# Attention, a routed expert layer and a gated network in one kernel: gathers, copies and stores reordered around the experts, and a second PSUM tile for the attention's product

## The chip, the cores and the metric

One Trainium2 chip; the kernel runs on one of its cores. Time is device time in microseconds (us). Engines: PE (TensorE, matrix products), DVE (VectorE), ACT (ScalarE), POOL (GpSimd) and SP (SyncE, which issues DMAs). Each engine works through its own instructions in order and waits on semaphores for the others.

## The reference

Three layers, each on the result of the one before. N is 4608 tokens (8 batches of 576), 512 wide.

```python
# attention: q, k, v are (8, 8, 576, 64)
q_s = softmax(q, axis=-1)              # exp(q - max) / (sum + 1e-9)
k_s = softmax(k, axis=2)               # over the sequence
kv  = einsum('bhsd,bhse->bhde', k_s, v)
x   = einsum('bhsd,bhde->bhse', q_s, kv)      # then (4608, 512)
# routed experts: E = 8, F = 1024, two experts for each token
logits = x @ w_gate + log1p(exp(x @ w_noise)) * noise
top2   = the two largest of each row; top2_w = softmax over the two
x      = sum over the two: top2_w * (relu(x @ w1[e]) @ w2[e])
# gated network
out = ((x @ w1) * (x @ w2)) @ w3 @ w_out
```

## The kernel before

Large products are done in split form: each float32 operand is the sum of a rounded part and a remainder (split(), L93: one ACT copy, one DVE subtraction), and mm3() (L97 to L100) adds three products.

**Attention and routing (front(), L142 to L593).** Tokens go in 36 tiles of 128. For tile i, q_tr transposes (L336), q_exp takes the exponential (eqT, L340), q_mm multiplies with the batch's table (pm, L347 to L350), q_out normalises (qr L355, xn L358, lp L360, xt L363) and stores the rows to X in device memory (L366). pm is one PSUM tile of two banks. Between these steps k_step prepares the tables of later batches. route() works out, for groups of tiles, the two experts of each token and its place in their lists, by one-hot products (L406, L464). As long as no expert works (alone is true, until the first 18 tiles are routed), bank() gives the transposes banks of ptr and pyy in turn, two each, and the routing's sums the two banks of phh. Afterwards the experts have phh and bank() gives all of the front ptr and pyy. The order of instructions on each engine up to L872 comes from the framework's planner, from dependences, the order of the text and its estimates; from L872 on (manual_schedule) it is the order of the text.

**Experts.** Expert 0's first-half tokens are done beside the rest of the attention (units 0 and 1, na = 2), then experts 1 to 7 in four units each (units 2 to 29), then expert 0's second half (units 30 and 31; nu = 32). A unit is two or three tiles of 128 rows: product1 (eight steps fb, result to a bank named ph, emptied by ACT L738 and DVE L739 into hT), then product2 (row blocks m, bank py, emptied by ACT L749, stored to Y in device memory by a DMA that ACT issues, L751). The rows of a unit are gathered from X by indirect DMAs of POOL (L709, or L137 in four quarters). Up to unit 2, transp() first copies the gathered rows into another column order (G.tensor_copy, L122, into a tile of the two-buffer pool y, which also holds the rows on their way to Y), then PE transposes (L124); later units are transposed by DVE in 32 x 32 blocks (L117). A hook after each step converts weights of the gated network on DVE and ACT (L628 to L646).

**Gated network (gated(), L993).** Blocks of three tiles: eight steps fb with two products of 12 matmuls each, then three row blocks m. take(i) (L953) weighs and adds the two expert rows of tile i (L957, L960), transposes and splits them into xT, and issues gather2(i + 2). gather2(i) fetches both expert rows of tile i from Y, eight indirect DMAs of POOL, into pool g2 with four buffers, two tiles deep. In block b, take() of block b + 1 comes after fb = 1, fb = 5 and m = 0 (CFB). The first takes come through events: take(0) after step 9 of unit 30, take(1) after step 2 and take(2) after step 7 of unit 31 (steps 0 to 7 are fb, 8 on are m). columns(), after unit 5, clamps pos (L879), lets PE replicate pos and gw over the partitions (replicate, L127 to L133) and writes posq and gwq (L880, L882), which gather2 and take use.

Of the kernel before, what the change touches and what calls it, by code (L numbers as in the profile page):

```python
# [8 lines left out]
F32 = mybir.dt.float32  # L9
# [6 lines left out]
ALU = mybir.AluOpType  # L16
AX = mybir.AxisListType
PSUM = bass.MemoryType.PSUM
# [7 lines left out]
E = 8  # L26
# [10 lines left out]
RTAIL = 4  # L37
PUMP = 3
CFB = {1: 0, 5: 1, 8: 2}
GROUPS = [(0, 9), (9, 15), (15, 18), (18, 26), (26, 32), (32, 35), (35, 36)]  # L40


@with_exitstack
def moe_chain_kernel(ctx, tc, q, kt, v0, v1, noise, wg, w1, w2, mw1, mw2, mw3t, mwo, out):
# [4 lines left out]
    def pool(stack, name, bufs, **kw):  # L49
        return stack.enter_context(tc.tile_pool(name=name, bufs=bufs, **kw))  # L50
# [33 lines left out]

    def open_late():
        early.close()
        for name, bufs in (("w2", 4), ("ht", 1), ("xt", 2), ("xg", 3), ("y", 2)):
            late[name] = pool(main, name + "p", bufs, side="right", reuse_waits="tile")
    ptr = pool(main, "ptr", 2, space=PSUM)
    phh = pool(main, "phh", 2, space=PSUM)  # L90
    pyy = pool(main, "pyy", 2, space=PSUM)

    def split(src, hi, lo):  # L93
        A.copy(out=hi, in_=src)  # L94
# [4 lines left out]
        P.matmul(ps, st_h, mv_l, start=False, stop=False)  # L99
        P.matmul(ps, st_l, mv_h, start=False, stop=last)  # L100

    turns = {"ph": [phh], "py": [pyy]}

    def bank_of(kind, shape):
        pools = turns[kind]
# [5 lines left out]

        return rows.rearrange("p (i c d) -> p c i d", i=4, c=4)

    def transp(src, xt, t, quarters):
        if quarters:
            pt = extra["xq"].tile([128, 4, 4, 32], F32, name="xq", tag="xq")
            V.transpose(out=pt, in_=src.rearrange("p (j c d) -> p c j d", j=4, c=4))  # L117
            pt = pt.rearrange("p c j t -> p c (j t)")
        else:
            pt = ptr.tile([128, 4, 128], F32, name="pt", tag="pt")  # L120
            rows = late["y"].tile([128, 4, 4, 32], F32, name="xr", tag="y")
            G.tensor_copy(out=rows, in_=by_chunk(src))  # L122
            for c in range(4):
                P.transpose(pt[:, c, :], rows[:, c].rearrange("p i d -> p (i d)"), ident)  # L124
        split(pt, xt[:, 0, :, 128 * t:128 * t + 128], xt[:, 1, :, 128 * t:128 * t + 128])
# [16 lines left out]
    def front(st):  # L142
# [9 lines left out]
        kts, vs, ks_, eks, qs, eqs, xq = {}, {}, {}, {}, {}, {}, {}  # L152
        alone = [True, 0]

        def bank(shape, route=False):
            if alone[0]:
                if route:
                    return phh.tile(shape, F32, name="rb", tag="ph")
                alone[1] += 1
                pl, tg = ((ptr, "pt"), (pyy, "py"))[alone[1] % 2]  # L160
                return pl.tile(shape, F32, name="fb", tag=tg)
            alone[1] += 1
            if alone[1] % 3 == 0:
                return pyy.tile(shape, F32, name="rb", tag="py")
            return ptr.tile(shape, F32, name="pt", tag="pt")
# [174 lines left out]
            A.activation(out=eqT, in_=pts.pop(i), func=AF.Exp)  # L340

        def q_mm(i):
            pms[i] = pm = pmm.tile([128, 4, 256], F32, name="pm", tag="pm")
            b0, b1 = (i * 128) // S, (i * 128 + 127) // S
            for p in range(4):
                if b0 == b1:
                    P.matmul(pm[:, p, 0:162], eqs[i][:, p, :], tab[b0 % 3][:, p, :], start=True, stop=True)  # L347
                else:
                    P.matmul(pm[0:64, p, 0:162], eqs[i][:, p, 0:64], tab[b0 % 3][:, p, :], start=True, stop=True)
                    P.matmul(pm[64:128, p, 0:162], eqs[i][:, p, 64:128], tab[b1 % 3][:, p, :], start=True, stop=True)  # L350
# [20 lines left out]
        def onehots(i0, sl, cols, acc):  # L371
            n, kk = sl.shape[1], sl.shape[2]
            si = sm.tile([128, n, kk], I32, name="si", tag="si")
            V.tensor_copy(out=si, in_=sl)
            yield
            sj = sm.tile([128, n, kk], I32, name="sj", tag="sj")
            V.tensor_single_scalar(out=sj, in_=si, scalar=7, op=ALU.arith_shift_right)
            V.tensor_single_scalar(out=si, in_=si, scalar=127, op=ALU.bitwise_and)
            yield
            jf = sm.tile([128, n, kk], F32, name="jf", tag="jf")  # L380
            V.tensor_copy(out=jf, in_=sj)
            pf = sm.tile([128, n, kk], F32, name="pf", tag="pf")
            V.tensor_copy(out=pf, in_=si)
            yield
            per = 4 // kk
            for c0 in range(0, n, 2 * per):
                c1 = min(n, c0 + 2 * per)
                pl = bank([128, cols], True)
                for a in range(c0, c1, per):
                    z = min(c1, a + per)  # L390
                    m = (z - a) * kk
                    oa = sm.tile([128, 4, 128], F16, name="oa", tag="oa")
                    V.tensor_tensor(out=oa[:, 0:m], in0=iob[:, None, :].to_broadcast([128, m, 128]),
                                    in1=pf[:, a:z, :].rearrange("p n k -> p (n k)")[:, :, None].to_broadcast(
                                        [128, m, 128]), op=ALU.is_equal)
                    yield
                    ob = sm.tile([128, 4, cols], F16, name="ob", tag="ob")
                    V.tensor_tensor(out=ob[:, 0:m], in0=iob[:, None, 0:cols].to_broadcast([128, m, cols]),
                                    in1=jf[:, a:z, :].rearrange("p n k -> p (n k)")[:, :, None].to_broadcast(
                                        [128, m, cols]), op=ALU.is_equal)  # L400
                    obn = ob[:, 0:m].rearrange("p (n k) c -> p n k c", k=kk)
                    G.tensor_tensor(out=obn, in0=obn, in1=tag[:, i0 + a:i0 + z][:, :, None, None].to_broadcast(
                        [128, z - a, kk, cols]), op=ALU.mult)
                    yield
                    for j in range(m):
                        P.matmul(pl, oa[:, j], ob[:, j], start=(a == c0 and j == 0), stop=(z == c1 and j == m - 1))  # L406
                    yield
                if i0 + c0 in (0, HT):
                    V.tensor_copy(out=acc, in_=pl)
                else:  # L410
                    V.tensor_tensor(out=acc, in0=acc, in1=pl, op=ALU.add)
                yield
# [17 lines left out]
        def route(gi):  # L430
# [29 lines left out]
            m = sm.tile([128, n, E], BF16, name="m", tag="m")  # L460
            V.tensor_tensor(out=m, in0=oh[:, :, 0, :], in1=oh[:, :, 1, :], op=ALU.add)
            yield
            pr = bank([128, n, E], True)
            P.matmul(pr, upper, m, start=True, stop=False)  # L464
            P.matmul(pr, onesb, run[:, None, :].to_broadcast([128, n, E]), start=False, stop=(n == 1))
            for j in range(n - 1):
# [46 lines left out]
            yield  # L513
            V.tensor_tensor(out=gw[:, i0:i1, 1], in0=gw[:, i0:i1, 0], in1=w, op=ALU.mult)
            if i1 in (HT, NT):
                pc = bank([128, E], True)
                P.matmul(pc, onesb, run, start=True, stop=True)
                V.tensor_copy(out=cnt[:, half, :], in_=pc)
                yield
# [198 lines left out]
    def xpose(u, t):  # L718
        if t == 0:
            xts[u] = late["xt"].tile([128, 2, 4, 384], F32R, name="xT", tag="xT")  # L720
        transp(xg.pop((u, t)), xts[u], t, u > na)

    def turn(u, step):
        n, e, part, j0, nt, N, first, last = units[u]
# [151 lines left out]

    def columns():

        V.tensor_scalar(out=pos, in0=pos, scalar1=float(E * ROWS - 1), scalar2=None, op0=ALU.min)  # L879
        V.tensor_scalar(out=posq, in0=replicate(pos.rearrange("p n k -> p (n k)")), scalar1=4.0,  # L880
                        scalar2=quart[:, 0:1], op0=ALU.mult, op1=ALU.add)
        V.tensor_copy(out=gwq, in_=replicate(gw.rearrange("p n k -> p (n k)")))  # L882
# [62 lines left out]
    def gather2(i):  # L945
        if i >= NT:
            return
        for k in range(2):
            y = extra["g2"].tile([128, D], F32, name="yg", tag="yg")
            gather_quarters(y, Y, posq[:, :, 2 * i + k:2 * i + k + 1])  # L950
            x2s[i, k] = y

    def take(i):  # L953
# [8 lines left out]
        b, t = divmod(i, BT)  # L962
        if t == 0:
            xts["g", b] = late["xt"].tile([128, 2, 4, 384], F32R, name="xT", tag="xT")
        transp(y0, xts["g", b], t, True)
        gather2(i + 2)

    def load_b():
        for j in range(4):
# [1 line left out]

    nu = len(units)
    events[nu - 3, 7] = [w34_begin]
    events[nu - 2, 9] = [lambda: take(0)]
    events[nu - 1, 2] = [lambda: take(1)]
    events[nu - 1, 7] = [lambda: take(2), load_b]
    for u in range(na, nu):
# [3 lines left out]
            unit(u, hook_conv, True)  # L981
        if u == na:
            turns["py"].append(ptr)
        if u == na + 3:
            columns()
        if u == nu - 3:
            w34()
    for j in range(4):
        wscratch(("w", j), 20 + j, late["w2"])

    most = nc.values_load(nmax[0:1, 0:1], min_val=0, max_val=T)

    def gated():  # L993
        N = 128 * BT
        nblk = NT // BT
        ap_ = extra["a"]
        for b in range(nblk):
            xt = xts.pop(("g", b))
            pT = late["ht"].tile([128, 2, 8, 384], F32R, name="hT", tag="hT")
            for fb in range(8):  # L1000
                f0 = 128 * (fb % 2)
                for g in ("a", "b"):
# [8 lines left out]
                    else:  # L1011
                        V.tensor_tensor(out=a, in0=a, in1=ps, op=ALU.mult)  # L1012
                        split(a, pT[:, 0, fb, :], pT[:, 1, fb, :])
                if b + 1 < nblk and fb in CFB:
                    take(BT * (b + 1) + CFB[fb])
            for m in range(BT):
                po = bank_of("py", [128, 512])
                for fb in range(8):
# [4 lines left out]
                A.copy(out=y, in_=po)  # L1023
                r = N * b + 128 * m
                nc.sync.dma_start(out=out[r:r + 128, :], in_=y)
                if b + 1 < nblk and m + 8 in CFB:
                    take(BT * (b + 1) + CFB[m + 8])

    gated()
    main.close()  # L1030
# [125 lines left out]
```

## Time and profile before

| | us |
|---|---|
| median of 3 runs | 1745.32 (1743.0 to 1746.36) |
| the profiled execution | 1746.65 |
| its span, first to last instruction | 1744.7 |
| PE busy | 1665.7 (95%) |
| DVE busy | 886.3 (51%) |
| ACT busy | 572.5 (33%) |
| POOL busy | 690.7 (40%) |
| mean granted TensorE clock | 0.982 |

A row of a timeline has the start, the length and the instruction, with out<-in by the program's names; in brackets stands the time for which the engine was idle before it, and what released it. Matmuls are pipelined: their lengths overlap, and the distance between their starts is what one takes. The front takes about 230 us, units 2 to 29 go to about 1020 us, the product of w3 and w_out (w34) and units 30 and 31 to about 1131, and the gated network takes the rest.

### The profile page before, as it was taken

The numbers are of one execution on the slowest core, as the hardware profiler recorded it, in microseconds if no ns is written. First come the engines' busy times: TensorE is split into PE (matmuls) and PEld (weight loads), VectorE is DVE, ScalarE is ACT, GpSimd is POOL, SyncE is SP. The second block draws the span as 40 slices with busy tenths as digits, with TensorE's granted clock in tenths as the row PEclk, the third lists the DMA queues.
The fourth block names the chain that finished last, engine by engine and source line by source line (L and its number), as shares of the span: only waits on it lengthen the run. The fifth ranks groups of instructions, "written<-read, shape, count | busy, mean of one in ns | idle before, by whom it ended". The sixth has DMA issues, their size and how long they took to land. (4 is left out here: it accounts for less than half of the span.)

```text
span 1744.7 us, 26430 instructions
## 1 busy us (share of the span) xinstructions
PE 1665.7 (95%) x9903; PEld 1519.5 (87%) x9903; DVE 886.3 (51%) x2251; ACT 572.5 (33%) x1195; POOL 690.7 (40%) x706
## 2 busy tenths in 40 slices
PE   6887979989999999999999999899999999999998
PEld 5666868988989989899998988789999999999997
DVE  6699735766567575774767513233323233332321
ACT  6553322333233333332333312232223233232321
POOL 4456334414334143341443420544454454444500
PEclk9898989999999999999999999999999999999999
DMA  8875344535355253553545484521111111111100
GB/s 297 263 238 173 110 151 150 175 104 168 112 169 172 86 177 124 162 157 104 166 152 173 154 318 165 187 101 43 49 53 48 52 54 35 44 48 52 50 23 20
DMA packets 130060, 221.51 MB, mean 127 GB/s; under 512 B 18560, under 2 KB 65792, under 8 KB 126848
## 3 DMA queue, kind: packets, MB, share of 16 engines
q1 hardware_dynamic: 95040, 152.07, 26.7%
q0 software_dynamic: 19072, 39.88, 8.4%
q10 hardware_dynamic: 15808, 27.71, 4.3%
q8 instruction: 85, 1.39, 0.3%
q14 instruction: 55, 0.45, 0.1%
HBM read 152.22 MB, written 67.37 MB: 126 GB/s over the span
## 5 line engine op out<-in xcount | busy, mean ns | idle before, releaser
L98 PE MATMUL ph<-xT,w 128*128 128x384 f32 (+1 forms) x1792 | 576.2, 322 | 13.6 <-DVE hT L739 9.4
L99 PE MATMUL ph<-xT,w 128*128 128x384 f32 (+1 forms) x1792 | 574.6, 321 | 0.8 <-DVE xT L95 0.7
L100 PE MATMUL ph<-xT,w 128*128 128x384 f32 (+1 forms) x1792 | 574.0, 320 | 0.0
L137 POOL DMA_INDIRECT xg<-X,idxq x288 | 282.5, 981 | 467.7 <-DVE xq L117 395.3
L137 POOL DMA_INDIRECT yg<-Y,posq x288 | 295.0, 1024 | 364.9 <-DVE yg L960 209.0
L98 PEld LDWEIGHTS ph<-xT,w 128*128 128x128 f32 x1792 | 339.8, 190 | 18.6 <-DVE hT L739 11.8
L100 PE MATMUL py<-w,hT 128*128 128x512 f32 x904 | 353.0, 390 | 0.4
L99 PE MATMUL py<-w,hT 128*128 128x512 f32 x904 | 352.3, 390 | 0.0
L98 PE MATMUL py<-w,hT 128*128 128x512 f32 x904 | 352.2, 390 | 0.0
L99 PEld LDWEIGHTS ph<-xT,w 128*128 128x128 f32 x1792 | 339.4, 189 | 3.3 <-DVE xT L95 1.5
L100 PEld LDWEIGHTS ph<-xT,w 128*128 128x128 f32 x1792 | 339.5, 189 | 0.0
L100 PEld LDWEIGHTS py<-w,hT 128*128 128x128 f32 x904 | 169.7, 188 | 37.4 <-DVE hT L739 2.0
L99 PEld LDWEIGHTS py<-w,hT 128*128 128x128 f32 x904 | 169.7, 188 | 34.0
L98 PEld LDWEIGHTS py<-w,hT 128*128 128x128 f32 x904 | 169.7, 188 | 33.9
L1012 DVE TENSOR_TENSOR a<-a,ph 128x384 f32<-128x384 f32 x96 | 53.0, 552 | 281.6 <-PE ph L100 263.5
L739 DVE SCALAR_TENSOR_TENSOR hT<-ph,hT 128x256 fp32r<-128x256 f32 (+1 forms) x256 | 120.5, 474 | 103.4 <-ACT hT L738 100.4
L738 ACT ACTIVATE hT<-ph 128x256 fp32r<-128x256 f32 (+1 forms) x256 | 107.2, 426 | 158.1 <-PE ph L100 143.6
L95 DVE TENSOR_TENSOR xT<-xq,xT 128x512 fp32r<-128x512 f32 x108 | 74.8, 693 | 154.9 <-ACT xT L94 154.9
L749 ACT COPY y<-py 128x512 f32<-128x512 f32 x77 | 45.2, 587 | 258.0 <-PE py L100 214.4
L94 ACT CAST xT<-xq 128x512 fp32r<-128x512 f32 x108 | 67.0, 620 | 138.7 <-DVE xq L117 129.2
L94 ACT CAST hT<-a 128x384 fp32r<-128x384 f32 x96 | 49.4, 514 | 182.3 <-DVE a L1012 182.3
L95 DVE TENSOR_TENSOR w<-raw,w 128x1024 fp32r<-128x1024 f32 x72 | 88.8, 1236 | 11.7 <-ACT w L94 11.6
(203 smaller groups left out, 1529.5 us busy)
## 6 DMA issues: line engine op xcount, KB each, us to landing
raw<-in_w_dram SPq DMA_DIRECT2D x72, 512.0 KB, 4.1
w<-WS SPq DMA_DIRECT2D x24, 1024.0 KB, 6.6
WS<-hl SPq DMA_DIRECT2D x80, 256.0 KB, 2.8
Y<-y ACTq DMA_DIRECT2D x77, 256.0 KB, 2.5
k<-in_kt_dram SPq DMA_DIRECT2D x32, 288.0 KB, 4.4
q<-in_q_dram SPq DMA_DIRECT2D x36, 256.0 KB, 4.0
X<-xt SPq DMA_DIRECT2D x36, 256.0 KB, 2.4
out_dram<-y SPq DMA_DIRECT2D x36, 256.0 KB, 2.1
```

The source lines that it names most:

```text
L94: A.copy(out=hi, in_=src)
L95: V.tensor_tensor(out=lo, in0=src, in1=hi.bitcast(F32), op=ALU.subtract)
L98: P.matmul(ps, st_h, mv_h, start=first, stop=False)
L99: P.matmul(ps, st_h, mv_l, start=False, stop=False)
L100: P.matmul(ps, st_l, mv_h, start=False, stop=last)
L137: G.indirect_dma_start(out=dst[:, 128 * j:128 * j + 128], out_offset=None, in_=src[:].rearrange("t (i c) -> (t i) c", i=4), in_offset=bass ...
L738: A.activation(out=hT[:, 0, fb, :N], in_=ph[:, :N], func=AF.Relu)
L739: V.scalar_tensor_tensor(out=hT[:, 1, fb, :N], in0=ph[:, :N], scalar=0.0, in1=hT[:, 0, fb, :N].bitcast(F32), op0=ALU.max, op1=ALU.subtract)
L749: A.copy(out=by_chunk(y), in_=py.rearrange("p (c i d) -> p c i d", c=4, i=4))
L1012: V.tensor_tensor(out=a, in0=a, in1=ps, op=ALU.mult)
```

## The change

The second pair of banks for pm, in the attention, as long as alone is true: pm2 takes the room of phh, which is opened when the experts begin, and the routing's sums go to the banks of the transposes. The copy ahead of the transposes goes from POOL to ACT (units 0 and 1) and to DVE (unit 2). The clamp of pos moves from columns() to the end of unit 2. The first takes issue no gathers; gather2(2) comes after step 4 of unit 30, into a raw tile, and gather2(3) and gather2(4) after unit 31. In block 0 of the gated network the takes come after fb = 4, fb = 7 and m = 1 (CF0).

```diff
+CF0 = {4: 0, 7: 1, 9: 2}
     def open_late():
         early.close()
+        turns["ph"].append(pool(main, "phh", 2, space=PSUM, side="right", reuse_waits="tile"))
...
-    phh = pool(main, "phh", 2, space=PSUM)
     pyy = pool(main, "pyy", 2, space=PSUM)
+    pm2 = pool(early, "pm2", 1, space=PSUM, side="right")
...
-    turns = {"ph": [phh], "py": [pyy]}
+    turns = {"ph": [], "py": [pyy]}
...
-    def transp(src, xt, t, quarters):
-        if quarters:
+    def transp(src, xt, t, straight):
+        if straight is None:
...
-            G.tensor_copy(out=rows, in_=by_chunk(src))
+            straight(out=rows, in_=by_chunk(src))
...
-        def bank(shape, route=False):
+        def bank(shape):
             if alone[0]:
-                if route:
-                    return phh.tile(shape, F32, name="rb", tag="ph")
...
-            pms[i] = pm = pmm.tile([128, 4, 256], F32, name="pm", tag="pm")
+            pms[i] = pm = (pm2 if alone[0] and i % 2 else pmm).tile([128, 4, 256], F32, name="pm", tag="pm")
...
-        transp(xg.pop((u, t)), xts[u], t, u > na)
+        transp(xg.pop((u, t)), xts[u], t, None if u > na else V.tensor_copy if u == na else A.copy)
...
     def columns():
-        V.tensor_scalar(out=pos, in0=pos, scalar1=float(E * ROWS - 1), scalar2=None, op0=ALU.min)
...
     def gather2(i):
+        if i == 2:
+            raw = rawp.tile([128, 2, D], F32, name="raw", tag="raw")
         for k in range(2):
-            y = extra["g2"].tile([128, D], F32, name="yg", tag="yg")
+            y = raw[:, k] if i == 2 else extra["g2"].tile([128, D], F32, name="yg", tag="yg")
...
     def take(i):
-        gather2(i + 2)
+        if i >= BT:
+            gather2(i + 2)
...
+    events[nu - 2, 4] = [lambda: gather2(2)]
     events[nu - 2, 9] = [lambda: take(0)]
...
         if u == na:
             turns["py"].append(ptr)
+            V.tensor_scalar(out=pos, in0=pos, scalar1=float(E * ROWS - 1), scalar2=None, op0=ALU.min)
...
     for j in range(4):
         wscratch(("w", j), 20 + j, late["w2"])
+    gather2(3)
+    gather2(4)
...
         for b in range(nblk):
+            turn_at = CFB if b else CF0
...
-                if b + 1 < nblk and fb in CFB:
-                    take(BT * (b + 1) + CFB[fb])
+                if b + 1 < nblk and fb in turn_at:
+                    take(BT * (b + 1) + turn_at[fb])
...
-                if b + 1 < nblk and m + 8 in CFB:
-                    take(BT * (b + 1) + CFB[m + 8])
+                if b + 1 < nblk and m + 8 in turn_at:
+                    take(BT * (b + 1) + turn_at[m + 8])
```

## Rows read from the trace of the kernel before

**Rows 1.** Busy time by stretch: us, PE, PEld, DVE, ACT, POOL (instructions), PEclk, DMA share, GB/s

```profile
70.00:130.00 60.00, 47.53 (x473) 40.14 (x474) 56.01 (x235) 36.33 (x78) 29.51 (x31) 0.94 0.75 248
...
372.10:378.80 6.70, 5.97 (x76) 5.81 (x77) 1.52 (x5) 0.00 (x0) 0.00 (x0) 0.50 0.29 87
379.00:1105.00 726.00, 725.39 (x4093) 656.23 (x4091) 428.30 (x998) 233.00 (x456) 252.47 (x258) 1.00 0.50 158
1109.40:1116.10 6.70, 3.95 (x18) 3.95 (x19) 3.71 (x10) 3.26 (x10) 1.72 (x2) 0.50 0.20 71
1143.50:1146.80 3.30, 3.30 (x12) 3.30 (x11) 2.69 (x8) 1.75 (x6) 0.11 (x1) 0.50 0.00 0
```

**Rows 2.** The chain that ended last, 1094 to 1143 us: start, us, what

```profile
1095.13 1.29 ACT yg L957 x4
...
1106.81 3.90 DMA yg<-Y,posq
...
1110.88 0.33 ACTq L751
...
1133.78 5.91 DMA yg<-Y,posq
...
1139.79 0.33 ACTq L751
```

**Rows 3.** Timeline of PE, 1105 to 1150 us: start, us, instruction, [idle before <-releaser]

```profile
1112.15 0.58 PE L98 MATMUL ph<-xT,w 128*128 128x256 f32 x1 [7.00 <-DVE hT L739]
...
1142.10 0.44 PE L98 MATMUL ph<-xT,w 128*128 128x384 f32 x1 [2.90 <-ACT a L1010]
...
1147.07 0.34 PE L99 MATMUL ph<-xT,w 128*128 128x384 f32 x1
...
1148.11 0.34 PE L99 MATMUL ph<-xT,w 128*128 128x384 f32 x1
```

**Rows 4.** Timeline of POOL, 1094 to 1147 us

```profile
1098.07 0.94 POOL L137 DMA_INDIRECT yg<-Y,posq  x1 [47.45 <-DVE xq L117]
```

**Rows 5.** Stores of Y, 248 to 255 us, from issue to landing

```profile
DMA to landing us min/median/max: 2.1/2.1/2.1
```

**Rows 6.** Timeline of PE, 367 to 380 us

```profile
372.83 1.19 PE L132 MATMUL py<-pos,ident 128*32 128x72 f32 x32 [4.72 <-DVE pos L879]
```

**Rows 7.** Timeline of POOL, 238 to 285 us

```profile
253.70 0.62 POOL L122 COPY xr<-xg 128x512 f32<-128x512 f32 x1
...
259.32 0.61 POOL L122 COPY xr<-xg 128x512 f32<-128x512 f32 x1
```

**Rows 8.** Timeline of ACT, 242 to 268 us

```profile
248.87 0.33 ACTq L751 DMA_DIRECT2D Y<-y  x1
```

**Rows 9.** Timeline of DVE, 238 to 285 us

```profile
256.15 0.69 DVE L95 TENSOR_TENSOR xT<-pt,xT 128x512 fp32r<-128x512 f32 x1 [5.38 <-ACT xT L94]
```

**Rows 10.** Timeline of PE, 238 to 300 us

```profile
261.79 0.69 PE L98 MATMUL ph<-xT,w 128*128 128x384 f32 x1 [0.68 <-ACT xT L94]
```

**Rows 11.** Line L637, all its instructions: ns min/median/max, first and last start, forms

```profile
L637 DVE TENSOR_SCALAR b<-mf x80: 281/286/417, 280.4 to 964.7; 128x256 int32<-128x256 int32 x80
```

**Rows 12.** Timeline of DVE, 133 to 150 us

```profile
135.09 3.25 DVE L269 TENSOR_SCALAR ks<-ks 128x4 f32<-128x4 f32 x1
```

**Rows 13.** Waits of PE, whole span: us in total, times, longest us

```profile
PE pt L124 <- POOL xr L122: 10.0, 3, 5.0
```

**Rows 14.** Waits of PE, 20 to 130 us

```profile
PE pm L347 <- DVE lp L360: 9.9, 7, 3.0
...
PE fb L252 <- ACT ek L255: 1.7, 2, 1.3
PE fb L252 <- ACT eqT L340: 1.6, 4, 0.7
```

**Rows 15.** Waits of ACT, 20 to 130 us

```profile
ACT xn L358 <- POOL xt L363: 12.9, 10, 3.3
```

**Rows 16.** Waits of DVE, 20 to 130 us

```profile
DVE qr L355 <- PE pm L347: 10.7, 11, 2.3
```

More of the change, by code (lines that the diff above doesn't have):

```diff
@@ L387, in onehots @@
                 c1 = min(n, c0 + 2 * per)
-                pl = bank([128, cols], True)
+                pl = bank([128, cols])
                 for a in range(c0, c1, per):
@@ L462, in route @@
             yield
-            pr = bank([128, n, E], True)
+            pr = bank([128, n, E])
             P.matmul(pr, upper, m, start=True, stop=False)
@@ L515, in route @@
             if i1 in (HT, NT):
-                pc = bank([128, E], True)
+                pc = bank([128, E])
                 P.matmul(pc, onesb, run, start=True, stop=True)
@@ L964, in take @@
             xts["g", b] = late["xt"].tile([128, 2, 4, 384], F32R, name="xT", tag="xT")
-        transp(y0, xts["g", b], t, True)
-        gather2(i + 2)
+        transp(y0, xts["g", b], t, None)
+        if i >= BT:
+            gather2(i + 2)
     def load_b():
```

## The prediction

> **What bounds the kernel now.** I read the busy time by stretch first, then the timelines and the chain where PE stands still, then the waits in the attention. In [rows 1] the reader is to see that from 379 to 1105 us PE is busy 725.4 of 726.0 us at the full clock. What is taken off another engine there is worth nothing; time can be won only where PE stands still, or where it works at the granted clock 0.50 (1.2 GHz, the lower of its two levels) after standing still. Behind the attention there are three such places: before 262 us, at 368 to 379, and at 1105 to 1147. In the attention itself DVE is busy 56.0 of 60.0 us between 70 and 130 us, PE 47.5 [rows 1]: there PE follows DVE. The sum is made against the profiled execution, 1746.65 us (span 1744.7); the median of the three runs, 1745.32, is 1.3 below it, and I take that off at the end.
>
> **The gathers of Y and the stores of Y (13.5 us).** From 1095 us on the chain [rows 2] runs through POOL's gathers from Y (L137) and not through PE. Each take() issues gather2(i + 2), eight gathers, ahead of later stores into Y. The next store (L751, on ACT) waits until these gathers have read Y, as the order is kept for Y as a whole: the last of eight starts at 1106.81 and lands 3.90 us later, and the store leaves at 1110.88. ACT stands behind its store, no bank of ph is emptied, and PE waits 7.00 us [rows 3]. The gathers of tiles 3 and 4 do it again: the last starts at 1133.78, needs 5.91 us, the store leaves at 1139.79, and PE waits 2.90. At clock 0.50 PE then worked 3.95 and 3.30 us [rows 1]; at the full clock half of that would do, so 3.6 is lost. 7.00 + 2.90 + 3.6 = 13.5.
>
> After the change the same eight gathers of tile 2 stand at step 4 of unit 30, ahead of all its stores, and go into a raw tile that the weights no longer need. POOL sat idle for 47.45 us before 1098.07 [rows 4], so they land long before the first of these stores. The gathers of tiles 3 and 4 stand behind the last store, and no store into Y follows. All 13.5 goes. They wait for that store now, and behind them on POOL stand only the gathers of the next tiles. What is late next: call E the end of the experts' last product. The last store can land by E + 4 (estimate: copy and issue, and 2.1 us of landing as in [rows 5]); from the first to the last of eight gathers pass 8.7 us [rows 2, 4], the last needs up to 5.9: tile 3 is there by E + 19. It is taken after the fifth step of the first block; a step is 24 products at 0.173 us (six in 1.04 us [rows 3]), 4.2 us, so at E + 21. Tile 4 is there by E + 29 and taken at E + 33. Tile 5, whose gathers follow the take of tile 3, is there by E + 40 and taken behind m = 1, at E + 45. A take occupies ACT and DVE for some 4 us (2.9 of them from 1095.13 to 1098.07 [rows 2, 4]), and 5.5 us (24 products a third wider) remain until block 1 wants it. All fits, the first and the last narrowly. Bounds: 10 (a take late by 3.5) to 13.5; I take 13.5, since the four ph banks cover four runs of 12 products, 8.3 us.
>
> **The clamp of pos (7.7 us).** At the end of the expert at 368 us PE replicates pos, and waits 4.72 us [rows 6] for a small DVE instruction (L879) that stands behind the conversions of the second network's weights. Between 372.1 and 378.8 PE then worked 5.97 us at clock 0.50 [rows 1]: 3.0 lost. Moved behind unit 2, the clamp is done three units earlier, and replicate() finds pos. posq and gwq stay behind the conversions on DVE, but their readers, the gathers of Y, come at the end of the experts, and the two banks they hold are wanted again only after eight runs of 12 products. Late next is DVE itself, some 5 us behind PE when the next unit starts; its four ph banks cover 8.3 us. Bounds: 4.7 (the clock falls anyway) to 7.7; I take 7.7.
>
> **The copies ahead of the transposes (5.1 us).** Unit 2's rows are put in order by POOL (L122). The second copy starts at 253.70 and the third at 259.32 [rows 7], because four gathers of the next unit stand on POOL between each two. On DVE no gather stands between. The second copy then waits for its buffer alone, that of the row block whose store left at 248.87 [rows 8] and landed 2.1 us later [rows 5]: 251.0. In program order DVE goes on with the second tile's split, which ended 3.14 us after its copy began (253.70 to 256.84 [rows 7, 9]), so the third copy starts at 254.2; from its start to the first product of unit 2 pass 2.47 us (259.32 to 261.79 [rows 7, 10]). Product at 256.7 instead of 261.8: 5.1. Were the third copy put ahead of the second split: 7.6. A copy of this form on DVE is not in the trace; I take the 0.6 of POOL's, between 0.3 (L637, half as wide [rows 11]) and 0.7. The clock falls either way.
>
> Does POOL hold up a DVE copy? While POOL ran its own tensor instructions back to back, a DVE instruction on four columns took 3.25 us [rows 12]; L637, many of whose 80 lay beside gathers, never took more than 0.42 us against 0.29 in the median [rows 11]. The Trainium skill (SBUF — State Buffer, Who interferes with whom) says that a VectorE copy from SBUF to SBUF in a two-port mode and a GpSimd instruction lock each other out for a whole instruction, whichever comes second. By that rule each of the later two copies would wait for up to one gather instruction, 0.94 us [rows 4], and 3.2 would remain of the 5.1. I go by L637 and keep 3.2 as the lower end.
>
> For units 0 and 1 the copy goes to ACT, 0.6 us each, five in all. PE's three waits for such a copy [rows 13] are all unit 2's, so nothing is won by it; where ACT's copy stands ahead of its gather's landing, the attention's instructions behind it on ACT wait. I take nothing, and count it in the lower end below.
>
> **The attention (3 us).** PE waits 9.9 us in seven waits for the one pair of banks of pm (L347 on DVE lp [rows 14]). A second pair takes these away. But ACT's copy xn waits 12.9 us for POOL's xt, whose single buffer waits for its store [rows 15], and that chain does not care about pm. What DVE can win is its own wait for the product, 10.7 us in eleven waits [rows 16], the upper end. Between 70 and 130 us DVE was idle for 4.0 us in all [rows 1], the row nearest to what is free to win. Against it: the routing's sums leave phh and share four banks with the transposes. PE's waits for ACT to empty such banks were 3.3 us (L252 [rows 14]); half as much again, with a gather awaited on ACT for 3.9 us [rows 2], would turn 1 into −5, the lower end. I take 4 − 1 = +3.
>
> Sum: 13.5 + 7.7 + 5.1 + 3 = 29.3; 1746.65 − 29.3 − 1.3 = 1716.
>
> **Rivals.** A second pair of pm is worth all that DVE waits for it: 10.7 instead of 3, so 1708. For it: ACT's and PE's waits hang together with pm. Against: xt's store, and DVE's 93% from 70 to 130. The Trainium skill (Perfetto Trace Analysis, Optimization Strategy) says that the same gap repeating on an engine that should be saturated can mean too little PSUM for the next tile. The seven waits look so, but PE is not the saturated engine here.
>
> Shared banks, or another order of the attention's instructions (a planner orders them, not the hand), cost 5 net instead of winning 3: 1724. For it: each of the four banks is held until ACT empties it. Against: only 3.3 us of such waits now.
>
> The gathers' wait moves instead of going: block 1 waits for the whole take of tile 5, 4 us, and PE works at clock 0.50 after it, 3 us lost as at 368: 1723. For it: 1 to 2 us of room. Against: lateness up to now was set by stores, and none is left.
>
> Slower than before: a routing sum holds its bank through several rounds of DVE and POOL while PE, in order, stands at the next transpose. Routing begins after nine tiles and the four banks are all there is until the 18th is listed, so nine tiles bear it. It decides if each takes over 3.3 us longer (29.3 − 3 + 3.5 = 30 over nine). At 4 us a tile, 36: 1746.65 − 26.3 + 36 − 1.3 = 1755. For it: DVE, at 93%, already feeds these sums late. Against: banks waited for so far cost 3.3 us over all tiles.
>
> **How the numbers follow.** Forecast 0.59, its own range 1711 to 1722; more from pm 0.14; shared banks 0.13; moved wait 0.06; slower 0.05. The lower ends of all four (10, 4.7, 3.2, −5) give 1732, the upper (13.5, 7.7, 7.6, 10.7) 1706; not all low at once: 1706 to 1730. A difference under 0.2% (3.5 us) is about what a measurement of this kernel can't tell from none; that needs three of the four gains to fail, 0.03. Faster 0.92, slower 0.05.
>
> **What would show it.** Right: no PE wait over 1 us between 1090 and 1150 and stores of Y right behind their copies; no wait at replicate(pos); about 5 us less between unit 1's last product and unit 2's first, with DVE copies between; pm's waits gone and DVE hardly less idle. Wrong: PE waits on ACT or DVE in the first block of the second network or before its block 1; waits on banks named fb in the attention; unit 0 starting later than now.

## The result and the profile after

The changed kernel takes 1724.48 us (median of 4 runs, 1722.57 to 1726.3) against 1744.73 for the one before (4 runs, 1743.0 to 1746.36): ratio 0.9884, 95% interval 0.9867 to 0.9901, or 20.3 us faster by the medians. The forecast was 1716, 1706 to 1730, faster: the time lies in the range and on the side forecast, 8.5 us above the point.

The profiled execution has a span of 1720.4 us, 24.3 less than before; that is 4 us more than the medians give, since it is the shortest of the four and the profiled one before (1746.65) lies above its median. To see where the 24 us are, I matched the n-th matmul of each kind in both traces from unit 2 on, where PE's order is the same, and took the difference after minus before along the way:

| place | before, us | after, us | gained in this stretch |
|---|---|---|---|
| unit 1's last product ends | 248.2 | 253.1 | −4.9 (attention) |
| unit 2's first product starts | 261.8 | 258.6 | 8.1 (the gap is 5.5 instead of 13.6) |
| behind unit 5, after replicate | | | 8.1 (0.9 up to 283 us, 7.2 at replicate) |
| block 0 of the gated network | | | 13.4 |
| from there to the end of the span | 1744.7 | 1720.4 | none |

The gains less the loss make 24.7; the 0.4 beyond the 24.3 is drift along the units between. Three of the four terms are there, and none under its forecast by more than half a microsecond. The fourth, the attention, has the other sign.

A second execution of the changed kernel was traced as well (span 1728.3, below). From unit 2's first product to the end it took 1463.2 us, the first trace 1461.8, the kernel before 1482.9, and its gap ahead of unit 2 is 5.5 us again. But unit 1's last product ends only at 259.7 us there. So the gains from the gap on repeat, and the size of the loss in the attention does not.

PE's share by stretch in the changed kernel, in the columns of [rows 1]:

```profile
362.00:379.00 17.00, 17.00 (x153) 16.23 (x152) 15.64 (x38) 8.24 (x14) 3.77 (x4) 1.00 0.62 192
1070.00:1130.00 60.00, 60.00 (x340) 55.24 (x340) 17.54 (x38) 16.87 (x40) 8.63 (x9) 1.00 0.47 172
1116.00:1150.00 34.00, 34.00 (x188) 33.02 (x187) 13.18 (x27) 10.62 (x25) 23.02 (x24) 1.00 0.28 91
1150.00:1200.00 50.00, 50.00 (x264) 47.22 (x263) 16.27 (x34) 14.90 (x34) 32.47 (x33) 1.00 0.21 60
```

The stretches hold what [rows 3] and [rows 6] were of: the replicate of pos, the end of the experts, block 0; the last one holds the start of block 1, at 1160.8 us. PE is busy in all of each at granted clock 1.00; before, it stood still for 4.72, 7.00 and 2.90 us in the first three and then worked at 0.50 [rows 1]. PE's timeline at replicate, answering to [rows 6]:

```profile
364.31 0.71 PE L134 MATMUL py<-pos,ident 128*32 128x72 f32 x32
364.83 0.68 PE L134 MATMUL py<-gw,ident 128*32 128x72 f32 x32
```

No bracket stands behind them: nothing was waited for. ACT's stores into Y and its weighing of the first tiles (timeline of ACT, 1072 to 1150 us), where [rows 2] had a store that stood behind gathers:

```profile
1084.19 1.28 ACT L958 ACTIVATE yg<-yg,gwq 128x128 f32<-128x128 f32 x4 [0.40 <-ACT y L749]
1089.26 0.33 ACTq L751 DMA_DIRECT2D Y<-y  x1
1093.12 1.27 ACT L958 ACTIVATE yg<-yg,gwq 128x128 f32<-128x128 f32 x4
1105.93 0.33 ACTq L751 DMA_DIRECT2D Y<-y  x1
1111.37 0.33 ACTq L751 DMA_DIRECT2D Y<-y  x1
...
1133.03 1.28 ACT L958 ACTIVATE yg<-yg,gwq 128x128 f32<-128x128 f32 x4
1145.76 1.28 ACT L958 ACTIVATE yg<-yg,gwq 128x128 f32<-128x128 f32 x4
```

The last two stores come 5.44 us apart, at the pace of the products. And POOL's gathers of tile 2 (into raw) and the first of tile 3 (timeline of POOL, 1030 to 1130 us):

```profile
1060.66 0.94 POOL L139 DMA_INDIRECT raw<-Y,posq  x1 [20.91 <-DVE w L97]
...
1070.00 0.94 POOL L139 DMA_INDIRECT raw<-Y,posq  x1 [0.30 <-issue]
1119.98 0.94 POOL L139 DMA_INDIRECT yg<-Y,posq  x1 [49.03 <-DVE a L1019]
```

The gathers of tile 2 are all issued 8.4 us before the store at 1078.37 that would have had to wait for them, and those of tile 3 start only after the last store at 1111.37.

Ahead of unit 2 the copies stand on DVE (timeline of DVE, 250 to 260 us; before, they were the rows of POOL in [rows 7]):

```profile
253.16 0.43 DVE L124 COPY xr<-xg 128x512 f32<-128x512 f32 x1 [5.76 <-DMA Y<-y]
254.34 0.43 DVE L124 COPY xr<-xg 128x512 f32<-128x512 f32 x1 [0.75 <-PE pt L126]
...
256.13 0.69 DVE L97 TENSOR_TENSOR xT<-pt,xT 128x512 fp32r<-128x512 f32 x1 [0.48 <-ACT xT L96]
256.74 0.42 DVE L124 COPY xr<-xg 128x512 f32<-128x512 f32 x1
```

and POOL at the same time:

```profile
253.86 1.02 POOL L139 DMA_INDIRECT xg<-X,idxq  x1 [14.92 <-DVE xr L124]
255.19 0.95 POOL L139 DMA_INDIRECT xg<-X,idxq  x1 [0.30 <-issue]
256.44 0.95 POOL L139 DMA_INDIRECT xg<-X,idxq  x1 [0.30 <-DMA xg<-X,idxq]
```

The second and third copies run while POOL is inside a gather, and take what the first takes beside an idle POOL: 0.43, 0.43, 0.42 us. The third stands right behind the second tile's split (256.13 + 0.69), as forecast.

In the attention, DVE's waits from 20 to 130 us, answering to [rows 16]:

```profile
DVE lp L360 <- ACT xn L358: 8.6, 9, 2.8
DVE qr L355 <- POOL xt L363: 7.8, 5, 2.0
DVE ks L269 <- ACT k L246: 4.4, 2, 3.9
DVE qr L355 <- PE pm L347: 2.3, 1, 2.3
```

The wait for pm fell from 10.7 to 2.3 us. The waits for ACT's xn and POOL's xt stand in its place: before, xn was 2.9 us in six waits in the same view, and xt was not listed. ACT's own wait for xt, answering to [rows 15], is as long as it was:

```profile
ACT xn L358 <- POOL xt L363: 13.0, 8, 5.0
```

The second traced execution, with the same order of instructions, has pm's wait back, in three pieces (DVE's waits from 20 to 130 us):

```profile
DVE qr L355 <- PE pm L347: 8.9, 3, 4.0
DVE qr L355 <- POOL xt L363: 7.1, 4, 2.7
DVE lp L360 <- ACT xn L358: 5.9, 7, 1.6
```

What the two have in common is the sum: DVE stands idle for 28.4 and 29.4 of these 110 us, before for 23.9, and in the eight traces here with the attention as before for 21.6 to 26.2.

### The profile page after: what moved, and what is told of

It is laid out like the page before. It is cut to its first block, busy times and chain, and to the rows that moved or that the text cites. A ratio compares the mean times of both kernels' runs of the same rounds, so it can differ in the third digit from the quotient of the medians.

```text
span 1720.4 us, 26408 instructions
## 1 busy us (share of the span) xinstructions
PE 1661.5 (97%) x9903; PEld 1514.6 (88%) x9903; DVE 880.6 (51%) x2254; ACT 574.7 (33%) x1200; POOL 683.7 (40%) x698
## 5 line engine op out<-in xcount | busy, mean ns | idle before, releaser
L139 POOL DMA_INDIRECT yg<-Y,posq x280 | 285.2, 1019 | 330.1 <-DVE yg L961 174.1
L739 DVE SCALAR_TENSOR_TENSOR hT<-ph,hT 128x256 fp32r<-128x256 f32 (+1 forms) x256 | 120.7, 474 | 89.2 <-ACT hT L738 86.0
L97 DVE TENSOR_TENSOR w<-raw,w 128x1024 fp32r<-128x1024 f32 x72 | 88.5, 1229 | 13.5 <-ACT w L96 13.1
```

Source lines behind the costliest of these rows:

```text
L97: V.tensor_tensor(out=lo, in0=src, in1=hi.bitcast(F32), op=ALU.subtract)
L139: G.indirect_dma_start(out=dst[:, 128 * j:128 * j + 128], out_offset=None, in_=src[:].rearrange("t (i c) -> (t i) c", i=4), in_offset=bass ...
L739: V.scalar_tensor_tensor(out=hT[:, 1, fb, :N], in0=ph[:, :N], scalar=0.0, in1=hT[:, 0, fb, :N].bitcast(F32), op0=ALU.max, op1=ALU.subtract)
```

## The experiments

In the first kernels a part is taken out of the changed kernel or varied; in the last four, one part is put into the kernel before. Ratios are to the kernel before, with 95% intervals.

**Taking the attention's part out.** phh is there from the start, the sums are in it, pm has its one pair; copies for units 0 and 1 on POOL as before.

```diff
-            pms[i] = pm = (pm2 if alone[0] and i % 2 else pmm).tile([128, 4, 256], F32, name="pm", tag="pm")
+            pms[i] = pm = pmm.tile([128, 4, 256], F32, name="pm", tag="pm")
-        def bank(shape):
+        def bank(shape, route=False):
             if alone[0]:
+                if route:
+                    return phh.tile(shape, F32, name="rb", tag="ph")
...
-        transp(xg.pop((u, t)), xts[u], t, None if u > na else V.tensor_copy if u == na else A.copy)
+        transp(xg.pop((u, t)), xts[u], t, None if u > na else V.tensor_copy if u == na else G.tensor_copy)
```

> The changed kernel with the attention as it was before: one pm, the routing's sums in phh, the copies of units 0 and 1 on POOL. Kept are DVE's copies for unit 2, the early clamp of pos and the moved gathers. Theory (the attention part of the change costs what the trace of after shows at 252 us, where unit 1 ends 4.9 us later than before): 4 to 8 us faster than the changed kernel's 1724.5, 1716 to 1720; the ratio to before 0.983 to 0.986. Rival (the 4.9 us are the scatter of single executions, and the attention part is worth nothing or the 3 us of the prediction): 1724 to 1728.

Measured: 1719.43 us, 0.9843 [0.9825, 0.9862], 26.6 us faster than the 1746.05 of its own comparison. Clamp, copies and gathers give more without the attention's part than the 0.9884 [0.9867, 0.9901] with it; against the changed kernel's second measurement, further on, the intervals overlap.

**The same, with the copies of units 0 and 1 left on ACT.**

> As the one with the whole attention undone, but the copies of units 0 and 1 stay on ACT. If the second pm and the shared banks cost the 4.9 us: within 1.5 us of that one. If the copies on ACT do, since ACT stands for a gather and the attention stands behind it: 3 to 6 us slower than that one, at the changed kernel's 1724.

Measured: 1718.97, 0.9838 [0.982, 0.9856]. The engine of these copies makes no difference that these runs show.

**The changed kernel with the copies of units 0 and 1 back on POOL** (A.copy becomes G.tensor_copy in the line above).

> The changed kernel, with the copies of units 0 and 1 back on POOL and nothing else undone. If the second pm and the shared banks cost the 4.9 us: 1724 as the changed kernel, within 1.5. If the copies on ACT cost it: 1718 to 1721.

Measured: 1722.26, 0.9858 [0.9839, 0.9876]. Its interval overlaps both that of the changed kernel and that of the run above: it settles nothing by itself.

**The changed kernel with one pm.** Two banks stay empty; the sums still share the transposes' four.

```diff
-            pms[i] = pm = (pm2 if alone[0] and i % 2 else pmm).tile([128, 4, 256], F32, name="pm", tag="pm")
+            pms[i] = pm = pmm.tile([128, 4, 256], F32, name="pm", tag="pm")
```

> The changed kernel with one pm in place of two; the two banks stay empty and the routing's sums still share the transposes' banks. If the shared banks are what costs, and the second pm wins something: 1 to 6 us slower than the changed kernel, 1725 to 1731. If the second pm itself costs, through the order of the instructions that the planner makes of it: 3 to 6 us faster, 1718 to 1721. If neither matters: 1724.

Measured: 1725.93, 0.9886 [0.9865, 0.9907], against 0.9838 with the sums in banks of their own: 7 us slower on the same chip, with no second pm in either. So a loss comes with the sums' move. What the second pm wins back is not settled: the kernels with shared sums and a second pm measure 0.9884, 0.9858 and, below, 0.9865, and all three intervals overlap this one. The traced execution of this kernel took 1721.86 us, 4.1 under its median, so its trace shows little of the loss.

**The changed kernel again**, beside the next kernels.

> The changed kernel itself, on the chip of the three that follow, for the comparison. If sharing the four banks costs what the runs so far say: 1722 to 1727, 4 to 7 us behind a kernel that differs in the attention alone. If the gap to those was the chip's or the executions' scatter: 1718 to 1721.

Measured: 1727.35, 0.9865 [0.9846, 0.9885], which is 23.6 us by this ratio's point, against 20.3 by the first.

**One pm, and transposes and sums together in all six banks** (ptr, pyy, phh), an edit of the kernel without the attention's part.

```diff
-                if route:
-                    return phh.tile(shape, F32, name="rb", tag="ph")
-                alone[1] += 1
-                pl, tg = ((ptr, "pt"), (pyy, "py"))[alone[1] % 2]
+                alone[1] += 1
+                pl, tg = ((ptr, "pt"), (pyy, "py"), (phh, "ph"))[alone[1] % 3]
```

> One pm; the routing's sums and the transposes share six banks in turn (ptr, pyy and phh) instead of four. If the four banks are too few for both: as the kernel with sums in banks of their own, 1717 to 1720. If a sum costs by standing in line with the transposes at all, or by the planner's order: as the one with four shared banks, 1723 to 1727.

Measured: 1728.42, 0.9886 [0.9868, 0.9905]. Six banks for the same tiles are no better than four. Too few banks is not the cause; what remains is that the sums stand in one rotation with the transposes, and that the planner then writes another order. These two weren't told apart by a run of their own; the traces say more, under the attention's part alone.

**No attention part, and the first two loads for the weights' conversion issued ahead of unit 2.** In the kernel without the attention's part DVE waits for one such load, while PE waits for DVE (waits of DVE, 262 to 280 us):

```profile
DVE ex L629 <- DMA cr<-in_mw_dram: 5.1, 1, 5.1
```

```diff
-    def conv_steps(cp):
-        pieces = list(conv_pieces())
-        raws = [conv_load(cp, p) for p in pieces[:2]]
+    def conv_steps(cp, pieces, raws):
...
-    conv = conv_steps(cp)
+    pieces = list(conv_pieces())
+    conv = conv_steps(cp, pieces, [conv_load(cp, p) for p in pieces[:2]])
```

> The changed kernel with the attention's one pm and the sums in phh (copies of units 0 and 1 on ACT), and the first two loads of the weight conversion put ahead of unit 2, so that DVE doesn't stand 4.9 us for them behind the first step of unit 2 and PE 2.4 us after it. If PE's wait goes with them: 2 to 4 us faster than the same without it, 1715 to 1717. If another wait takes its place (DVE has the next unit's splits and conversions to do at once): 1718 to 1719.

Measured: 1714.60, 0.9797 [0.9777, 0.9817]. From 262 to 280 us neither this wait of DVE nor PE's 2.4 us for hT is listed any more.

**The same, with unit 2's ordered rows in the pool of the later units' rows**, not in the pool that the rows on their way to Y use.

```diff
-            rows = late["y"].tile([128, 4, 4, 32], F32, name="xr", tag="y")
+            rows = (extra["xq"].tile([128, 4, 4, 32], F32, name="xq", tag="xq") if "xq" in extra else
+                    late["y"].tile([128, 4, 4, 32], F32, name="xr", tag="y"))
```

> The one with early conversion loads, and the ordered rows of unit 2 go to the two buffers of the later transposes (xq) instead of the pool y, so that they don't wait for the stores of Y. If the wait for the store (6.9 us idle on DVE before the first copy) sets unit 2's start: PE's gap of 5 us falls to 3 to 3.5, 1.5 to 2 us faster than without it. If PE's third transpose, which needs a bank back from ACT and DVE, sets it: under 1 us.

Measured: 1711.22 (1709.86 to 1712.69), 0.9782 [0.9765, 0.9798]: faster than the kernel before and the changed one. The step from the 1714.60 of the run above is not clear of noise by itself; the intervals overlap. PE's gap ahead of unit 2 is 3.3 us, and PE works on at the full clock, where the kernel with a gap of 5.1 fell to 0.50 (windows of the one with 5.1, then of this one):

```profile
255.00:260.00 5.00, 4.28 (x14) 3.67 (x13) 0.69 (x1) 0.59 (x1) 3.78 (x5) 0.50 0.18 54
```

```profile
255.00:260.00 5.00, 4.66 (x25) 4.41 (x26) 1.80 (x3) 1.43 (x3) 2.02 (x3) 1.00 0.15 39
```

**Each part alone, in the kernel before.** First the attention's part, with all its edits of the diff and no others.

> Before with the attention's part of the change alone: second pm from the banks of phh, phh opened after the attention, the sums in the banks of the transposes. Theory 1 (this part costs): the kernels with it took 1722 to 1728 us and the same kernel without it 1719, so it is 3 to 9 us slower than before, ratio 1.002 to 1.005, and unit 1's last product ends 3 to 9 us after the 248.2 of before. Theory 2 (the prediction: the second pm gains): 3 us faster, ratio 0.998, unit 1 ends near 245. Theory 3 (the shift at unit 1 is the scatter of single executions): ratio 0.999 to 1.001.

Measured: 1750.83, 1.0023 [1.0014, 1.0031]: 4.0 us slower. Unit 1's last product ends at 252.9 instead of 248.2. DVE's waits from 130 to 212 us:

```profile
DVE lacc L408 <- PE pt L405: 4.5, 2, 3.1
DVE lacc L410 <- PE pt L405: 3.5, 6, 1.4
DVE qr L354 <- PE pm L349: 2.4, 2, 2.1
```

and those of the kernel before in the same stretch:

```profile
DVE lacc L411 <- PE rb L406: 1.0, 2, 0.9
DVE lacc L409 <- PE pt L406: 0.6, 2, 0.3
...
DVE lacc L411 <- PE pt L406: 0.2, 1, 0.2
```

DVE waits 8.0 us for the sums' products instead of 1.8. PE in turn waits for what it multiplies there, POOL's ob, in the same stretch 7.6 us in six waits instead of 3.5 in six:

```profile
PE pt L405 <- POOL ob L401: 7.6, 6, 4.4
```

By these rows it is the operand of the sum that is late, not a bank that is full: PE stands at a product that can't run yet, with all its later work behind it. But these waits can't come from banks that the change made common. From about 130 us on alone is false, and both kernels give sums and transposes the same four banks by one rule: two tiles in ptr (here named pt), then one in pyy (named rb); pm has its one pair in both. The last one-hot sum before that and the first behind it (PE, 125 to 142 us, the kernel before, where the first row's rb is phh; then this one):

```profile
127.84 0.22 PE L406 MATMUL rb<-ob,oa 128*128 128x10 f16 x3 [1.12 <-POOL ob L402]
135.82 0.30 PE L406 MATMUL pt<-ob,oa 128*128 128x80 f16 x4 [0.68 <-POOL ob L402]
```

```profile
127.93 0.22 PE L405 MATMUL fb<-ob,oa 128*128 128x10 f16 x3 [1.25 <-POOL ob L401]
136.87 0.31 PE L405 MATMUL pt<-ob,oa 128*128 128x80 f16 x4
```

Up to there hardly any loss shows. The first list of tokens (idxa, L487 before, L486 here), with which the stretch of different banks closes, starts at nearly the same time (timelines of DVE, the kernel before, then this one):

```profile
129.92 0.17 DVE L487 CAST idxa<-lac 128x10 int32<-128x10 f32 x1
```

```profile
130.54 0.16 DVE L486 CAST idxa<-lac 128x10 int32<-128x10 f32 x1
```

Over all traces, idxa starts between 128.3 and 133.5 us in the eight whose attention is as before, and between 128.9 and 133.7 in the six with the sums moved. From idxa to the end of unit 1 the eight take 117.3 to 120.7 us, the four with the whole of the attention's part (the changed kernel's two among them) 122.3 to 126.0, six banks 126.6, and one pm 118.3 in the one execution traced. So most of the time is lost behind 130 us, where all have the same rule. What differs there is the order of the instructions (already up to idxa, DVE's is one and the same in the eight and another in the four) and where the turn of the banks stands: from 130 to 212 us, five of the fifteen groups of sums go to pyy before, none in this kernel.

How far the late operand carries, the other traces show. DVE's wait for the sums, in the same view, is 1.5 to 3.4 us in the eight and 5.8 to 8.0 in the four. But with moved sums and one pm (four banks or six) it is 2.9 and 3.0, and those two kernels took as long. PE's row alone separates less: 3.5 to 6.6 in the eight.

**The clamp alone** (it moves behind unit 2).

> Before with the clamp of pos alone moved ahead of the next unit. Theory 1 (the matmul of replicate waited for the clamp, and the gain stays): 7.2 to 7.7 us faster, ratio 0.9957, and no PE wait over 1 us near 368 us. Theory 2 (the wait only changes its name: DVE's queue, or the experts' tables that are due next, hold PE instead): within 2 us of before, ratio 0.999 to 1.001, with a new PE wait between 360 and 385.

Measured: 1737.1, 0.9951 [0.9936, 0.9965], 8.6 us faster. From 360 to 390 us PE is busy for all of it at the full clock (this kernel, then the one with the attention's part alone, whose clamp is where it was):

```profile
360.00:390.00 30.00, 30.00 (x215) 27.52 (x214) 25.05 (x60) 11.43 (x21) 7.67 (x9) 1.00 0.63 193
```

```profile
360.00:390.00 30.00, 25.27 (x178) 22.86 (x177) 17.42 (x43) 8.81 (x17) 5.86 (x7) 0.89 0.33 99
```

**Unit 2's copies alone on DVE.**

```diff
-    def transp(src, xt, t, quarters):
+    def transp(src, xt, t, quarters, straight=None):
...
-            G.tensor_copy(out=rows, in_=by_chunk(src))
+            (straight or G.tensor_copy)(out=rows, in_=by_chunk(src))
...
-        transp(xg.pop((u, t)), xts[u], t, u > na)
+        transp(xg.pop((u, t)), xts[u], t, u > na, V.tensor_copy if u == na else None)
```

> Before with unit 2's three copies on DVE instead of POOL, the buffers of them unchanged. Theory 1 (POOL's queue, with the 5.6 us copies and the gathers, set unit 2's start): PE's gap ahead of unit 2's first product falls from 13.6 to 5 to 6, 8 to 9 us faster with the 0.50 clock at 280 to 283 us gone, ratio 0.9950. Theory 2 (the gap was set by the store that the buffer waits for, and the copies' engine is beside the point): gap 11 to 13.6, gain under 3 us, ratio over 0.998.

Measured: 1736.57, 0.995 [0.9932, 0.9969], 8.7 us faster. The gap is 5.3 us. The second drop of the clock, which was to go, came all the same: 0.50 from 273.6 to 277.0 us. PE's waits from 245 to 300 us, where POOL's copies were 10.0 us in [rows 13]:

```profile
PE pt L124 <- DVE xr L122: 2.6, 3, 1.8
```

**The gathers and takes alone** (CF0, gather2 of tiles 2 to 4 and the raw tile, as in the change's diff).

> Before with the gathers and the takes of the last stage alone moved (second rows of blocks 0 and 1 gathered early, take points of block 0 at 4, 7, 9). Theory 1 (PE waited for the first block's rows, and that wait is gone): 13.4 us faster, ratio 0.9923, no PE wait over 1 us between 1070 and 1130. Theory 2 (the early gathers collide with the loads of the experts' last weights): under 10 us, ratio over 0.9943, with PE waits for weights before 1100.

Measured: 1732.41, 0.9923 [0.9907, 0.9938], 13.4 us faster. No wait of PE is left between 1070 and 1150 us:

```profile
1070.00:1150.00 80.00, 80.00 (x454) 75.24 (x454) 28.90 (x57) 26.55 (x58) 24.06 (x25) 1.00 0.44 161
```

## Why the prediction was right, and where it was not

**Gathers and stores of Y: right.** 13.5 forecast; 13.4 between the traces, and 13.4 [10.8, 16.2] alone. Both lost waits went, and the clock lost behind them came back. The rival in which the wait moves to block 1 is out: block 1 starts at 1160.8 us, and from 1150 to 1200 us PE is busy for 50.00 of 50.00 us.

**Clamp: right.** 7.7 forecast; 7.2 between the traces, 8.6 [6.1, 11.2] alone, of which some was won elsewhere (see the sum). DVE, named as late next, held nobody up.

**Copies: right in mechanism, mis-sized.** 5.1 forecast; 8.1 in the gap between the traces, as in the second trace, and 8.7 [5.4, 11.9] alone. Three steps of the sum differ. The second copy was put at 251.0, 2.8 us behind unit 1's end at 248.2, behind the store that left at 248.87 [rows 8]. It came 1.3 us behind unit 1's end (254.34 against 253.1) and waited for PE's transposes of the first tile; it is the first copy that waits for a store, an earlier one. A copy took 0.43 instead of the 0.6 assumed. And from the third copy's start to unit 2's first product it was 1.87 us (256.74 to 258.61), not 2.47. Nor did POOL hold a copy up: the second and third started inside gathers of 1.02 and 0.95 us and took 0.43 and 0.42. The Trainium skill (SBUF — State Buffer, Who interferes with whom) says that a VectorE copy in a two-port mode and a GpSimd instruction shut each other out for a whole instruction; the rows don't agree with such a lock for this pair, and don't show in which mode the copies ran.

**Attention: wrong in sign.** The step that failed reads "I take 4 − 1 = +3". What was measured is −4.0 [−5.4, −2.4] for this part alone, and −4.9 and −11.4 at unit 1's end in the two traces of the changed kernel.

The −1, the cost of the sums among the transposes, is the term that failed for certain: with one pm in both, moving the sums cost 7 us (1725.93 against 1718.97). It was sized by PE's waits for ACT to empty banks. The waits that came are of another kind: PE, in order, stands at a sum whose operand POOL has not finished, and DVE waits for that sum's product, 8.0 us instead of 1.8. The term's lower end was −5, and the rival that held this case, 1724, is near the time measured. Of its two mechanisms, banks held until ACT empties them is not borne out: six banks instead of four (0.9886) gained nothing, and most of the time is lost behind 130 us, where the rule for banks is the same again. The other, another order of the attention's instructions, fits: every kernel with moved sums has one. It is not shown as the cause. Where the turn of ptr and pyy stands differs too, no run changed the order or the turn alone, and the two kernels with one pm lost the time without DVE's long waits for the sums.

The 4 was what DVE could win when pm no longer holds it up. The traces don't show it. DVE's wait for pm fell by 8.4 us from 20 to 130 us in one trace of the changed kernel, by 1.8 in the other and by 6.5 with the part alone, and in all three the waits for xn and xt rose by more than that: together 2.9 before, then 16.4, 13.0 and 14.4. The chain of POOL's xt and its store, which the prediction itself said "does not care about pm", took the place. The tenth lp starts at 71.2, 75.5 and 72.5 us, against 69.3 before and 68.9 to 71.8 in the eight traces with the attention as before, so nothing was ahead by then. What a second pm is worth beside moved sums stays open all the same: by the ratios of the runs (0.9886 without it; 0.9884, 0.9865 and 0.9858 with it) it may be anything from nothing to some 5 us.

**The sum.** The four parts alone multiply to 0.9951 × 0.9950 × 0.9923 × 1.0023 = 0.9848; all together measure 0.9884 [0.9867, 0.9901] and 0.9865 [0.9846, 0.9885]. The three parts without the attention's multiply to 0.9825 and measure 0.9843 [0.9825, 0.9862]. In time the parts alone add up to 26.7 us (8.6 + 8.7 + 13.4 − 4.0), and together they gave 20.3 and 23.6. The intervals of five ratios together are wide, but the traces name places for a difference of this size: alone, each part also won time at stalls that belong to another part. Matched product by product, the clamp alone won 2.0 us in block 0, the copies alone 1.6 there and 1.2 at replicate, the gathers alone 1.3 at replicate. In block 0 the second wait was shorter (waits of PE, 1060 to 1160 us, clamp alone; 2.9 before):

```profile
PE ph L98 <- ACT a L1010: 1.7, 1, 1.7
```

At replicate PE waited 4.7 us as before, but the clock came back sooner (360 to 390 us, the kernel before, then copies alone):

```profile
360.00:390.00 30.00, 25.28 (x177) 23.39 (x176) 19.06 (x48) 9.22 (x16) 6.61 (x7) 0.89 0.43 131
```

```profile
360.00:390.00 30.00, 25.27 (x187) 23.75 (x186) 22.76 (x53) 10.02 (x18) 5.82 (x7) 0.94 0.54 169
```

These 6.1 us can't be had in the changed kernel, where neither stall is left. It is one trace of each part; that other executions win the same there is not shown. Single executions also scatter: in the five kernels whose front is as before, the front's last step (idx) starts between 229.4 and 233.1 us.

The gain forecast was 29.3 us, 9.0 more than the 20.3 of the result. The attention's term makes 7.0 of that (from +3 to −4.0). By their own runs, copies and clamp gave 3.6 and 0.9 more than forecast, which by the paragraph above counts some gains twice. The time lies in the range because the range allowed the attention a loss of 5. That the point is off by no more is in part luck: the copies, which gave more than forecast, made up for some of what the attention lost.

## What to carry to other kernels

Before a wait is priced as a gain, list what the waiting engine waits for next: a second buffer pays only as far as no other chain feeds the same instruction, and the sign of that is the engine's idle time, which did not fall here. A stall of an engine that works in order is best sought behind the instruction that heads its queue (a gather ahead of a store, a clamp behind conversions, a copy behind gathers): three such moves, which add no work, gave 26.6 us together here. Parts that were measured alone can't simply be added up: each can also win at a stall that another part removes. And the smallest part of a sum deserves its own run: the change without it, with an earlier load and another buffer for unit 2's rows, is the fastest kernel here, 1711.22 us.

## What was not expected of the hardware

A DVE copy of 128 x 512 float32 in another column order took 0.42 to 0.43 us, beside POOL's gathers as without them, where POOL took 0.61 to 0.62 for the same [rows 7]. After the gap of 5.5 us PE worked at granted clock 0.50 from 258.04 to 264.86 us, then at 1.00 to the end of the last products. In the second traced execution, after the same gap, it fell a second time, from 285.0 to 288.4 us, as it had before the change from 279.9 to 283.3. After a gap of 3.3 us, in the fastest kernel, it stayed at 1.00.
